# Keys of two groups in one product, and nine more score blocks on VectorE, in a gated mix of two attentions

## The chip, the cores and the metric

One core of a Trainium2 chip. The metric is the device time of one execution in microseconds (us); three executions gave a median of 815.02 (814.9 to 815.13). TensorE multiplies matrices into PSUM, ScalarE does the exponentials, VectorE and GpSimd the elementwise work, and DMAs are issued from SyncE's queue (SP) and GpSimd's.

## The reference

```python
x = A_x                                              # 1 x 2048 x 512, 32 heads of 16
g = _sigmoid((x * gate_w).sum(-1, keepdims=True))
a = _A_ref(x, A_wqkv, A_wo)                          # full attention
b = _B_ref(x, B_wqkv, B_wo)                          # each query sees 8 keys, at distance 0, 2, ... 14
return g * a + (1 - g) * b
```

with, in `_A_ref`,

```python
scores = jnp.einsum("bhqd,bhkd->bhqk", q, k) * (Dh ** -0.5)
p = _softmax(scores, axis=-1)
o = jnp.einsum("bhqk,bhkd->bhqd", p, v)
```

Attention A needs 32 x 2048 x 2048 exponentials. Attention B is small and is done beside it, for the most part on GpSimd.

## The kernel before

**Blocks and periods.** Attention A is cut into blocks: one head, 128 keys, 512 queries. Four heads form a group, and a group with one chunk of 512 queries is a period: 8 groups times 4 chunks are 32 periods of 64 blocks, in order of chunks and, within a chunk, of groups. A block is a score product (32 rows of the array, out of the key tile kt_all and the query tile qt), an exponential, and a value product (17 columns: 16 values and a one that gives the softmax's sum) into the period's accumulator in PSUM.

**Who does the exponential.** Most blocks go to ScalarE, in sets of three and two by turns: the scores land in PSUM rings, one ACTIVATE makes a set of pT from them (qk and ex, L1308 and L1314). `n_dve` (L20) says how many blocks of each period go to VectorE in place of that, in groups of three (d_set, L1218): per block one eviction that turns the scores into the bits of an approximate exponential (p1, tile dt_a or a part of wkv), per group three shifts of that tile (sh, tile pd_a), and per block four value products, with differently weighted values (vd_all), in place of one. In the first eight periods all groups share one buffer dt_a (NDE = 1, L45); later three are in use, two of them in the space of the weights wkv, which is free once all keys and values of attention A are made.

**Keys.** Groups 0 to 7 are needed one after the other in the first eight periods, and so are made along the way. For one group and one of four chunks of 512 keys, k_proj (L644) makes 16 products (mm_k, L378): four slices of x times four heads, each 32 columns wide, placed beside each other in the array. Columns 16 to 31 of a head hold the next head's keys (for the fourth head the group's first again, copied into wk3 by k3, L587). VectorE evicts the result into kt_all and takes the maximum of each row along (an operation that also writes an accumulator; rowc gives the sign). k_bound (L663) takes the maximum over the chunks, exchanges the halves of each head's 32 rows through two small products with permutation matrices (perm), negates, and fills the 16 rows beside each head's keys with the negative bounds. The query tile has the queries in 16 rows and their absolute values in the other 16, so that a score product gives the score less an upper bound of it.

**Queries.** The first two periods have their own product (q_proj). From the third on q_pair (L788) makes the queries of two groups in one full-width product, VectorE casts them (qs) and takes absolute values (qa), two stores put both into DRAM (q_scr, put), and a load for each period brings them into the layout of qt (get).

**Attention B.** b_tile (L880) makes keys, values and queries of 128 positions on TensorE, stores keys and values (kv_scr), gathers the eight neighbours (ksh, vsh, issued by SP) and multiplies and sums on GpSimd, 16 tiles in all.

**Order.** All work is a list of operations with an engine, a duration, a due time, dependencies and buffers; list_schedule (L175) plays it through, and the order in which it starts them becomes the program order of each engine. An operation with a smaller due time goes first; one that uses a shared PSUM bank gets a much earlier one. S0[p] is the planned start of period p (17 us and 0.465 us for each earlier block of ScalarE). Three PSUM banks serve all projections, the scores of VectorE's blocks and the accumulators, of which at most two are alive. The accumulator's transpose accT (po1, L1345) has a due time 100 us or more past everything else's (PO1D, L118). Where TensorE would be idle for too long, zeros (L1472) puts in products of a zero tile z.

Of the kernel before, what the change touches and what calls it, by code (L numbers as in the profile page):

```python
# [9 lines left out]
ALU = mybir.AluOpType  # L10
AX = mybir.AxisListType
FP32 = mybir.dt.float32
BF16 = mybir.dt.bfloat16
# [3 lines left out]

CFG = dict(
    set_sizes=(3, 2),
    n_dve=(3, 3, 6, 6, 6, 9, 9, 9) + (12,) * 24,  # L20
    dve_tiles=4,
    b_start=36.0,
    b_space=(44.0,) * 4 + (47.0,) * 4 + (49.0,) * 8,
# [4 lines left out]
DH = 16  # L28
NG = 8
W = 8  # L30
DIL = 2
QW = 512
# [4 lines left out]
DEXP = -2.0565  # L37
NV = 4
NGR = 3
ROW = QW + 2  # L40
NPT = 3
NGA = 3
# [9 lines left out]
def _ap(base, dims):  # L52
    return bass.AP(tensor=base.tensor, offset=base.offset, ap=[list(d) for d in dims])
# [53 lines left out]
SB = lambda n: [(True, 0.065 + n / 3840.0)]  # L107
# [4 lines left out]
WAVE = lambda n: PASS * n  # L112
# [189 lines left out]
def kernel(  # L302
# [26 lines left out]
    const = ctx.enter_context(tc.tile_pool(name="const", bufs=1))  # L329
# [37 lines left out]
    V = Chained(nc.vector, "dve")  # L367
    A = Chained(nc.scalar, "act")
    G = Chained(nc.gpsimd, "pool")
    SP = Chained(nc.sync, "sp")  # L370

    def mm(out, lhsT, rhs, start, stop, **kw):
        return chain(nc.tensor.matmul(out, lhsT=lhsT, rhs=rhs, start=start, stop=stop, **kw))  # L373
# [16 lines left out]
    def op(eng, occ, fn, dl, **kw):  # L390
        if any(tk.kind == "misc" for tk in kw.get("use", ())):
            dl -= URG[eng]
        o = Op(eng, occ, fn, dl, **kw)
        ops.append(o)
        return o
# [17 lines left out]
    n_dve = cfg["n_dve"]  # L413
# [43 lines left out]
    S0 = [T0 + UNIT * f for f in first_unit]  # L457

    wkv = const.tile([128, DC, 2 * D], BF16, name="wkv")
    wq = const.tile([128, DC, D], BF16, name="wq")  # L460
    wq2 = const.tile([128, DC, 8, 2, DH], BF16, name="wq2")
    q_scr = tc.dram_tile([NG * NC // 2 * 16, DH * QW], BF16, name="q_scr")
    wk3 = const.tile([128, DC, NG, 2, DH], BF16, name="wk3")
    a_w3 = A_wqkv.rearrange("(c p) n -> p c n", p=128)
    gw = const.tile([128, DC], BF16, name="gw")
    bw = const.tile([128, DC, 3 * D], BF16, name="bw")
    bwo = const.tile([128, DC, D], BF16, name="bwo")
# [7 lines left out]
    rowc = const.tile([128, 3], FP32, name="rowc")  # L475
    wts = const.tile([128, NV - 1], BF16, name="wts")
    z32 = const.tile([128, 32], BF16, name="z32")
    z_bc = _ap(z32[:, 0:1], [list(z32[:].ap[0]), [0, QW]])
    perm = const.tile([128, 2, 4, 2, DH], BF16, name="perm")
    qmask = const.tile([128, 1], U32, name="qmask")  # L480
    xT = const.tile([128, DC, S], BF16, name="xT")
    kt_all = const.tile([128, NG, S], BF16, name="kt_all")
    vp_all = const.tile([128, NT, H, DH + 1], BF16, name="vp_all")
    vd_all = const.tile([128, NV - 1, NTD, H, DH + 1], BF16, name="vd_all")
    kmax_all = const.tile([128, NG, NC], FP32, name="kmax_all")
    kmax_b = const.tile([128, NG], BF16, name="kmax_b")
    negk = const.tile([128, NG], FP32, name="negk")
# [29 lines left out]
    def init_perm():  # L517
        idv = ident[:].rearrange("p (a b d) -> p a b d", a=4, b=2)
        G.memset(perm[:], 0.0)
        G.tensor_copy(out=perm[:, 0, :, 1, :], in_=idv[:, :, 0, :])  # L520
        G.tensor_copy(out=perm[:, 1, 1:4, 1, :], in_=idv[:, 0:3, 1, :])
        G.tensor_copy(out=perm[:, 1, 0, 1, :], in_=idv[:, 3, 1, :])

    def init_pool2():
        make_identity(nc, identf)
# [11 lines left out]
    o_perm = op("pool", 1.0, init_perm, -8.5, deps=[o_id])  # L537
    o_init_p = op("pool", 2.8, init_pool2, -8.0, deps=[o_perm])
# [37 lines left out]
    o_wk = op("sp", 0.5, load_w(1), -8.9, lat=6.5)  # L576
# [10 lines left out]
    def k3(E, i0, i1):  # L587
        def s():
            wk = wkv[:, :, 0:D].rearrange("p c (i j d) -> p c i j d", i=NG, j=4)
            for e, j in ((0, 3), (1, 0)):  # L590
                E.tensor_copy(out=wk3[:, :, i0:i1, e, :], in_=wk[:, :, i0:i1, j, :])
        return s
# [6 lines left out]
        return s  # L599

    o_k3 = [op("dve", 0.2, k3(V, 0, 1), -4.0, deps=[o_wk])]
    o_k3 += [op("pool", 2.0, k3(G, 1, NG), -3.0, deps=[o_wk, o_init_p])] * (NG - 1)
    o_q2 = [op("dve", 0.5, q2(V, 0), 0.0, deps=[o_wq]), op("pool", 1.5, q2(G, 1), 5.0, deps=[o_wq, o_k3[1]])]

    def warm():
# [5 lines left out]
    o_xt = []  # L611
    for sc in range(NC):
        st = {}
# [76 lines left out]
            o_k[i] = [op("dve", 0.0, fill(0, S), dl, deps=[c], parts=SB(S))] * NC  # L690

    o_k = {}
    for i in range(NG):
        o_kc[i] = []
        for sc in range(NC):
            if i == 0:
                o_kc[i].append(k_proj(i, sc, ("misc", "acc", "misc", "misc")[sc], -2.0 + sc))
            else:
                o_kc[i].append(k_proj(i, sc, "misc", S0[i] - 14.0 - 3.5 * (NC - 1 - sc), rel=S0[i - 1] - 12.0 if i > 1 else K1REL))
        k_bound(i, 2.0 if i == 0 else S0[i] - 11.0)  # L700
# [87 lines left out]
    def q_pair(pi, dl, rel):  # L788

        c_, i = periods[pi]  # L790
        st = {}
        tk, tqs, tqa = tok("misc", 2), tok("qs", 1), tok("qa", 1)

        def part(c0, c1):
            def s():
                if c0 == 0:
                    st["p"] = misc_ps([128, QW])
                for c in range(c0, c1):
                    mm(st["p"][:], wq[:, c, 4 * i * DH:4 * (i + 2) * DH], xT[:, c, c_ * QW:(c_ + 1) * QW], c == 0, c == DC - 1)
            return s  # L800

        def ev():
            st["s"] = work.tile([128, QW], BF16, name="qs", tag="qs", bufs=1)
            V.tensor_copy(out=st["s"][:], in_=st["p"][:])

        def ab():
            st["a"] = work.tile([128, QW], BF16, name="qa", tag="qa", bufs=1)
            V.tensor_scalar(out=st["a"][:].bitcast(U32), in0=st["s"][:].bitcast(U32), scalar1=0x7FFF7FFF, scalar2=None,
                            op0=ALU.bitwise_and)

        def put(e):
            def s():
                src = st["sa"[e]]
                SP.dma_start(out=_ap(q_scr[8 * pi + e:8 * pi + e + 1, :], [[2 * DH * QW, 8], [QW, DH], [1, QW]]),
                             in_=src[:])
            return s

        def get(e):
            def s():
                qt_tiles[pi + e] = work.tile([128, QW], BF16, name="qt", tag="qt", bufs=4)  # L820
                SP.dma_start(out=qt_tiles[pi + e][:], in_=_ap(q_scr[8 * (pi + e):8 * (pi + e) + 1, :], [[QW, 128], [1, QW]]))
            return s
        a = op("pe", WAVE(2), part(0, 2), dl - 8.6, full=2, deps=[o_wq] + o_xt[c_], alloc=[tk], rel=rel, name=f"qp{pi}")
        a = op("pe", WAVE(2), part(2, DC), dl - 8.0, full=2, deps=[a], use=[tk], name=f"qp{pi}")
        c = op("dve", 0.61, ev, dl - 7.0, deps=[a], alloc=[tqs], use=[tk])
        b = op("dve", 0.0, ab, dl - 6.8, deps=[c], alloc=[tqa], use=[tqs], parts=SB(QW))
        w = [op("sp", 0.5, put(0), dl - 5.0, deps=[c], use=[tqs], lat=2.2), op("sp", 0.5, put(1), dl - 4.0, deps=[b], use=[tqa], lat=2.2)]
        for e in range(2):
            q_tok[pi + e] = tok("qt", 4)
            o_q[pi + e] = op("sp", 0.5, get(e), dl - 1.0 + e, deps=w, alloc=[q_tok[pi + e]], lat=2.2)  # L830
# [468 lines left out]
    for k, us in enumerate(sets):  # L1299
# [6 lines left out]
        st = dict(k=k, us=us, tn=tn, tp=tp)  # L1306
# [7 lines left out]
        def ex(st=st, n=n, k=k):  # L1314
# [4 lines left out]
        a = op("pe", 0.0, qk, tn - 3.0, mode="r", js=[u_[2] for u_ in us], deps=[o_q[pi] for pi in pis] + kd,  # L1319
               alloc=[tr_], use=[q_tok[pi] for pi in pis], after=[last_qk[0]], scores=k % 2, name=f"qk{k}")  # L1320
# [15 lines left out]
    for pi, (c_, i) in enumerate(periods):  # L1336
        st = {}
# [179 lines left out]
```

## Time and profile before

| | |
|---|---|
| median of three runs | 815.02 us |
| profiled execution | 816.37 us |
| its span, first to last instruction | 814.6 us |
| mean granted TensorE clock | 0.997 |
| first pT on ScalarE starts | 18.54 us |
| pT instructions on ScalarE | 778.7 us busy, 684 instructions, 1709 blocks |
| TensorE, products of the zero tile | 138.2 us, 425 |
| keys: products of wkv and of wk3 (tile wk) | 384 and 128 |
| evictions of keys out of PSUM | 32, from 10.0 to 197.2 us |

The profile's columns: a group line has the source line, engine, operation, output and input tiles with their shapes and count, then busy time and mean ns of one, then the idle time just ahead of them on their engine and what ended it. L364 and L373 are helpers that record every instruction, so the tile's name tells what a line is. Matmuls overlap: the start of the next one says more than the duration.

### The profile page before, as it was taken

The numbers are of one execution on the slowest core, as the hardware profiler recorded it, in microseconds if no ns is written. First come the engines' busy times: TensorE is split into PE (matmuls) and PEld (weight loads), VectorE is DVE, ScalarE is ACT, GpSimd is POOL, SyncE is SP. The second block draws the span as 40 slices with busy tenths as digits, with TensorE's granted clock in tenths as the row PEclk, the third lists the DMA queues.
The fourth block names the chain that finished last, engine by engine and source line by source line (L and its number), as shares of the span: only waits on it lengthen the run. The fifth ranks groups of instructions, "written<-read, shape, count | busy, mean of one in ns | idle before, by whom it ended". The sixth has DMA issues, their size and how long they took to land.

```text
span 814.6 us, 18016 instructions
## 1 busy us (share of the span) xinstructions
PE 754.1 (93%) x6969; PEld 247.2 (30%) x7022; DVE 685.0 (84%) x1068; ACT 786.8 (97%) x708; POOL 633.1 (78%) x1058
## 2 busy tenths in 40 slices
PE   8989999999999999989899999899989998999997
PEld 5343333323222222222232222223222222322322
DVE  5636787787988999989988899998989699999796
ACT  3999999999999999999999999999999999999996
POOL 3097979997998999999997894979789219998910
PEclk9999999999999999999999999999999999999999
DMA  8503081544344354444524516162442321522000
GB/s 261 140 5 118 2 180 42 149 111 104 93 100 127 104 118 130 110 112 107 132 54 111 136 33 163 34 162 54 91 130 50 81 86 58 144 59 72 1 2 27
DMA packets 58886, 77.22 MB, mean 95 GB/s; under 512 B 3744, under 2 KB 50848, under 8 KB 58800
## 3 DMA queue, kind: packets, MB, share of 16 engines
q1 hardware_dynamic: 52608, 53.91, 21.4%
q0 software_dynamic: 6048, 22.02, 14.8%
q8 instruction: 55, 0.90, 0.5%
q14 instruction: 31, 0.25, 0.1%
q10 hardware_dynamic: 144, 0.13, 0.0%
HBM read 43.78 MB, written 10.26 MB: 66 GB/s over the span
## 4 chain that ended last, share of the span: by engine, by line
ACT 49%; PE 24%; issue 21%; DVE 3%; DMA 2%; SPq 1%; ACTq 0%; DVEq 0%
ACT pT L364 48%; PE misc_ps L373 16%; PE ring L373 8%; DMA xld<-in_A_x_dram 1%; ACT lg L364 1%; SPq L364 1%; DMA woarr<-in_A_wo_dram 0%; DVE pd_a L364 0%; DMA q_scr<-qa 0%; DVE accT L364 0%; PE pxt L621 0%; DVE qs L364 0%; DVE qa L364 0%; DVE kt_all L364 0%; DVE kvs L364 0%
## 5 line engine op out<-in xcount | busy, mean ns | idle before, releaser
L364 ACT ACTIVATE pT<-ring 128x1536 bf16<-128x1536 f32 (+1 forms) x684 | 778.7, 1329 | 12.1 <-PE ring L373 9.3
L373 PE MATMUL ring<-qt,kt_all 32*128 32x512 bf16 x1709 | 268.7, 382 | 46.7 <-ACT pT L364 39.0
L364 POOL TENSOR_TENSOR prod<-ksh,qb 128x256 f32<-128x256 bf16 x256 | 174.0, 729 | 58.0 <-DMA ksh<-kv_scr 53.2
L373 PE MATMUL misc_ps<-pT,vp_all 128*17 128x512 bf16 (+1 forms) x1709 | 205.6, 384 | 1.7 <-DVE accT L364 1.1
L373 PEld LDWEIGHTS <-kt_all 32*128 32x128 bf16 x2048 | 88.2, 91 | 294.9 <-issue 286.4
L364 DVE TENSOR_SCALAR pd_a<-wkv 128x1536 uint16<-128x1536 uint16 x192 | 175.0, 941 | 0.9 <-PE misc_ps L373 0.4
L364 POOL TENSOR_TENSOR prod<-prod 128x256 f32<-128x256 f32 (+1 forms) x256 | 167.2, 668 | 5.6
L364 DVE TENSOR_SCALAR wkv<-misc_ps 128x512 uint16<-128x512 f32 x192 | 128.7, 683 | 26.8 <-PE misc_ps L373 24.1
L373 PE MATMUL misc_ps<-z 128*32 128x512 bf16 x425 | 138.2, 387 | 1.6 <-DVE z L364 1.6
L364 DVE TENSOR_SCALAR pd_a<-dt_a 128x1536 uint16<-128x1536 uint16 x147 | 135.2, 943 | 1.8 <-PE misc_ps L373 1.1
L373 PE MATMUL misc_ps<-pd_a,vd_all 128*17 128x512 bf16 x1017 | 130.9, 381 | 0.4 <-DVE pd_a L364 0.2
L373 PE MATMUL misc_ps<-qt,kt_all 32*128 32x512 bf16 x339 | 124.2, 381 | 1.3 <-DVE kt_all L364 0.4
L364 DVE TENSOR_SCALAR dt_a<-misc_ps 128x512 uint16<-128x512 f32 x147 | 98.8, 683 | 26.6 <-PE misc_ps L373 25.0
L364 POOL TENSOR_TENSOR prod<-vsh,lg 128x256 f32<-128x256 bf16 x128 | 84.2, 758 | 0.0
L373 PEld LDWEIGHTS <-vp_all 128*17 128x17 bf16 (+1 forms) x2048 | 55.1, 88 | 87.0 <-issue 73.2
L364 POOL TENSOR_TENSOR av<-vsh,lg 128x256 f32<-128x256 bf16 x128 | 78.2, 646 | 0.0
L373 PE MATMUL misc_ps<-bw,xT 128*128 128x512 bf16 x164 | 51.7, 389 | 1.1 <-issue 0.5
L373 PEld LDWEIGHTS <-z 128*32 128x32 bf16 x425 | 37.5, 96 | 48.2 <-issue 24.8
L373 PEld LDWEIGHTS <-vd_all 128*17 128x17 bf16 x1017 | 34.5, 88 | 48.2 <-issue 39.4
L373 PEld LDWEIGHTS <-xT 128*128 128x128 bf16 x576 | 29.1, 97 | 34.0 <-issue 31.0
L373 PE MATMUL misc_ps<-xT,wkv 128*32 128x512 bf16 x384 | 36.6, 381 | 0.0
L373 PE MATMUL misc_ps<-xT,wk 128*32 128x512 bf16 x128 | 35.8, 381 | 0.0
(89 smaller groups left out, 554.0 us busy)
## 6 DMA issues: line engine op xcount, KB each, us to landing
ksh<-kv_scr SPq DMA_DIRECT2D x32, 512.0 KB
vsh<-kv_scr SPq DMA_DIRECT2D x32, 512.0 KB
av<-prod POOLq DMA_DIRECT2D x28, 512.0 KB, 5.7
av<-av POOLq DMA_DIRECT2D x14, 512.0 KB, 5.3
kv_scr<-kvs SPq DMA_DIRECT2D x16, 256.0 KB
qt<-q_scr SPq DMA_DIRECT2D x30, 128.0 KB
q_scr<-qs SPq DMA_DIRECT2D x15, 128.0 KB
q_scr<-qa SPq DMA_DIRECT2D x15, 128.0 KB
```

The costliest lines, as they stand in the source:

```text
L364: return chain_on(key, f(*a, **k))
L373: return chain(nc.tensor.matmul(out, lhsT=lhsT, rhs=rhs, start=start, stop=stop, **kw))
```

## The change

Three things. The blocks of VectorE in the fifth to eighth period go from 6, 9, 9, 9 to 9, 9, 12, 12 (339 to 348 in all). The keys of groups 2 to 7 are made in pairs: the weights of two groups are interleaved into wkp by GpSimd at the start (per head position 16 columns of the one group, then 16 of the other), and one product, 128 columns wide, takes the place of eight. The eviction into the even group's tile is as before; the odd group's tile is made from that tile in SBUF, with the sign turned (KSB). One maximum covers both (so it is the largest absolute value), the exchange takes two small products for the pair, and then each group's tile gets its fill, in which the rows of the other group's keys are overwritten by the bounds. In the odd group the keys lie in the second 16 rows of each 32, so the queries and absolute values of odd groups are stored the other way round, which takes two stores of 64 partitions in place of one of 128.

```diff
-    n_dve=(3, 3, 6, 6, 6, 9, 9, 9) + (12,) * 24,
+    n_dve=(3, 3, 6, 6, 9, 9, 12, 12) + (12,) * 24,
...
+NK1 = 2
+KSB = True
+KPD, KPS, KPR, KP1, KP2 = 16.0, 3.5, 20.0, 44.0, 11.0
...
-    wk3 = const.tile([128, DC, NG, 2, DH], BF16, name="wk3")
+    wk3 = const.tile([128, DC, NK1, 2, DH], BF16, name="wk3")
+    wkp = const.tile([128, DC, (NG - NK1) // 2, 4, 2, DH], BF16, name="wkp")
...
-    perm = const.tile([128, 2, 4, 2, DH], BF16, name="perm")
+    perm = const.tile([128, 3, 4, 2, DH], BF16, name="perm")
...
+        G.tensor_copy(out=perm[:, 2, :, 0, :], in_=idv[:, :, 1, :])
...
-    o_k3 += [op("pool", 2.0, k3(G, 1, NG), -3.0, deps=[o_wk, o_init_p])] * (NG - 1)
+    o_k3 += [op("pool", 0.6, k3(G, 1, NK1), -3.0, deps=[o_wk, o_init_p])] * (NK1 - 1)
+
+    def kpw():
+        wk = wkv[:, :, 4 * NK1 * DH:D].rearrange("p c (i e j d) -> p c i e j d", e=2, j=4, d=DH)
+        for c in range(DC):
+            for e in range(2):
+                G.tensor_copy(out=wkp[:, c, :, :, e, :], in_=wk[:, c, :, e, :, :])
+    o_kp = op("pool", 2.0, kpw, 6.0, rel=12.0, deps=[o_wk, o_k3[1]])
...
+    def k_pair(i, dl, rel):
+        cs = []
+        for sc in range(NC):
+            st = {}
+            tk = tok("misc", 2)
+            def part(c0, c1, st=st, sc=sc):
+                def s():
+                    if c0 == 0:
+                        st["p"] = misc_ps([128, QW])
+                    for c in range(c0, c1):
+                        mm(st["p"][:], wkp[:, c, (i - NK1) // 2].rearrange("p j e d -> p (j e d)"), xT[:, c, sc * QW:(sc + 1) * QW],
+                           c == 0, c == DC - 1)
+                return s
+            def ev(e, st=st, sc=sc):
+                def s():
+                    src = kt_all[:, i, sc * QW:(sc + 1) * QW] if e and KSB else st["p"][:]
+                    V.tensor_scalar(out=kt_all[:, i + e, sc * QW:(sc + 1) * QW], in0=src, scalar1=(1.0, -1.0)[e], scalar2=None,
+                                    op0=ALU.mult, op1=ALU.max, accum_out=kmax_all[:, i + e, sc:sc + 1])
+                return s
+            d = dl - KPS * (NC - 1 - sc)
+            a = op("pe", WAVE(2), part(0, 2), d - 1.8, full=2, deps=[o_kp] + o_xt[sc], alloc=[tk], rel=rel, name=f"kp{i}.{sc}")
+            a = op("pe", WAVE(2), part(2, DC), d - 1.2, full=2, deps=[a], use=[tk], name=f"kp{i}.{sc}")
+            a = op("dve", 0.61, ev(0), d, deps=[a], use=[tk])
+            cs += [a, op("dve", 0.61, ev(1), d + 0.3, deps=[a], use=[] if KSB else [tk])]
...
+        def mx():
+            V.tensor_reduce(out=kmax_b[:, i:i + 1], in_=kmax_all[:, i:i + 2, :], axis=AX.XY, op=ALU.max)
+        def sw():
+            st["p"] = misc_ps([128, 2])
+            for e in range(2):
+                mm(st["p"][:, e:e + 1], perm[:, 2 * e].rearrange("p a b d -> p (a b d)"), kmax_b[:, i:i + 1], True, True)
+        def ng():
+            V.tensor_scalar(out=negk[:, i:i + 2], in0=st["p"][:], scalar1=-1.0, scalar2=None, op0=ALU.mult)
+        def fill(e):
+            def s():
+                V.tensor_scalar(out=kt_all[:, i + e, :], in0=kt_all[:, i + e, :], scalar1=rowc[:, 1 + e:2 + e],
+                                scalar2=negk[:, i + e:i + e + 1], op0=ALU.mult, op1=ALU.add)
+            return s
...
+        for e in range(2):
+            o_k[i + e] = [op("dve", 0.0, fill(e), dl + 3.0 + 20.0 * e, deps=[m], parts=SB(S))] * NC
+
+    for i in range(NK1, NG, 2):
+        k_pair(i, S0[i] - (KPD if i > 2 else KP2), S0[i - 1] - KPR if i > 2 else KP1)
+    for i in range(NK1):
...
         def put(e):
             def s():
                 src = st["sa"[e]]
+                if i < NK1:
-                SP.dma_start(out=_ap(q_scr[8 * pi + e:8 * pi + e + 1, :], [[2 * DH * QW, 8], [QW, DH], [1, QW]]),
-                             in_=src[:])
+                    SP.dma_start(out=_ap(q_scr[8 * pi + e:8 * pi + e + 1, :], [[2 * DH * QW, 8], [QW, DH], [1, QW]]),
+                                 in_=src[:])
+                    return
+                for g_ in range(2):
+                    r0 = 8 * (pi + g_) + (e ^ g_)
+                    SP.dma_start(out=_ap(q_scr[r0:r0 + 1, :], [[2 * DH * QW, 4], [QW, DH], [1, QW]]),
+                                 in_=src[64 * g_:64 * g_ + 64, :])
```

The due times of a pair: its last chunk is planned 16 us (11 for groups 2 and 3) ahead of the start of the even group's first period, and none of its products ahead of 20 us before the period in front (44 us for groups 2 and 3). Before, a group's last chunk was due 14 us ahead of its own period.

More of the change, by code (lines that the diff above doesn't have):

```diff
@@ L692 @@
     o_k = {}
-    for i in range(NG):
+    def k_pair(i, dl, rel):
[22 more added lines that the diff above has]
+            cs += [a, op("dve", 0.61, ev(1), d + 0.3, deps=[a], use=[] if KSB else [tk])]
+        st = {}
+        tk = tok("misc", 2)
+        def mx():
[11 more added lines that the diff above has]
+            return s
+        m = op("dve", 0.2, mx, dl + 0.5, deps=cs)
+        m = op("pe", 0.1, sw, dl + 1.0, full=0, deps=[m, o_perm], alloc=[tk])
+        m = op("dve", 0.2, ng, dl + 1.8, deps=[m], use=[tk])
+        for e in range(2):
+            o_k[i + e] = [op("dve", 0.0, fill(e), dl + 3.0 + 20.0 * e, deps=[m], parts=SB(S))] * NC
@@ L826, in q_pair @@
         b = op("dve", 0.0, ab, dl - 6.8, deps=[c], alloc=[tqa], use=[tqs], parts=SB(QW))
-        w = [op("sp", 0.5, put(0), dl - 5.0, deps=[c], use=[tqs], lat=2.2), op("sp", 0.5, put(1), dl - 4.0, deps=[b], use=[tqa], lat=2.2)]
+        np_ = 0.5 if i < NK1 else 1.0
+        w = [op("sp", np_, put(0), dl - 5.0, deps=[c], use=[tqs], lat=np_ + 1.7),
+             op("sp", np_, put(1), dl - 4.0, deps=[b], use=[tqa], lat=np_ + 1.7)]
         for e in range(2):
```

## The prediction

> **What bounds the kernel now.** I read the busy times first, then the span in stretches, then ScalarE's own timeline with its gaps, then what TensorE did just ahead of the gaps.
>
> The first line of the page says that ScalarE is the bound:
>
> ```profile
> PE 754.1 (93%) x6969; PEld 247.2 (30%) x7022; DVE 685.0 (84%) x1068; ACT 786.8 (97%) x708; POOL 633.1 (78%) x1058
> ```
>
> TensorE's 93% is softer than it looks: 138.2 us of it are fillers (the 425 products of the zero tile z). The stretches show when ScalarE is short of work (columns: stretch, length, busy us and count on PE, PEld, DVE, ACT, POOL, then granted clock, DMA share, GB/s):
>
> ```profile
> 100.00:125.00 25.00, 23.83 (x265) 8.21 (x263) 21.13 (x38) 23.52 (x22) 19.04 (x31) 1.00 0.69 159
> 150.00:175.00 25.00, 23.16 (x245) 7.14 (x240) 18.97 (x35) 23.49 (x23) 23.90 (x39) 0.93 0.50 109
> 225.00:250.00 25.00, 23.38 (x184) 6.65 (x186) 20.82 (x31) 25.00 (x24) 20.88 (x36) 1.00 0.54 137
> 275.00:300.00 25.00, 24.10 (x212) 7.25 (x213) 24.59 (x38) 24.95 (x24) 24.00 (x40) 1.00 0.64 148
> ```
>
> From 175 us on ScalarE has hardly a hole, though periods of 12 VectorE blocks run there. Before, it loses about a microsecond in each stretch. The holes on its timeline (start, length, instruction, idle before it and who ended that):
>
> ```profile
> 54.54 5.97 ACT L364 ACTIVATE pT<-ring 128x1536 bf16<-128x1536 f32 x5 [1.45 <-PE misc_ps L373]
> ...
> 83.37 6.89 ACT L364 ACTIVATE pT<-ring 128x1536 bf16<-128x1536 f32 x6 [0.86 <-PE ring L373]
> ...
> 107.27 2.37 ACT L364 ACTIVATE pT<-ring 128x1536 bf16<-128x1536 f32 x2 [1.19 <-PE ring L373]
> ...
> 136.59 13.66 ACT L364 ACTIVATE pT<-ring 128x1536 bf16<-128x1536 f32 x12 [1.00 <-PE ring L373]
> ...
> 167.97 12.87 ACT L364 ACTIVATE pT<-ring 128x1536 bf16<-128x1536 f32 x11 [1.38 <-PE ring L373]
> ```
>
> With two small ones (0.26 at 68.55, 0.29 at 112.56) that is 6.43 us in seven gaps, all ended by TensorE. Ahead of the gap at 136.59 TensorE was making keys:
>
> ```profile
> 134.49 0.58 PE L373 MATMUL misc_ps<-xT,wkv 128*32 128x512 bf16 x3
> 134.70 0.38 PE L373 MATMUL misc_ps<-xT,wk 128*32 128x512 bf16 x1
> 134.71 0.58 PE L373 MATMUL misc_ps<-xT,wkv 128*32 128x512 bf16 x3
> ...
> 136.09 0.60 PE L373 MATMUL ring<-qt,kt_all 32*128 32x512 bf16 x5
> ...
> 163.39 0.40 PE L373 MATMUL misc_ps<-pT,vp_all 128*32 128x512 bf16 x4 [1.10 <-DVE accT L364]
> ```
>
> Four products 32 wide run beside each other, and the next four start 0.22 us later (134.49 to 134.71). Eight such waves, group 5's last two chunks, fill 133.84 to 135.57, and only behind them come the scores that ScalarE waits for. The last line is another kind of gap: TensorE waits 1.10 us for VectorE's transpose accT, and then its clock halves:
>
> ```profile
> 164.00:166.00 2.00, 2.00 (x10) 0.35 (x7) 1.35 (x4) 1.89 (x3) 1.64 (x3) 0.56 0.84 129
> 166.00:168.00 2.00, 2.00 (x16) 0.32 (x15) 1.76 (x4) 0.62 (x2) 2.00 (x4) 0.59 0.28 94
> ```
>
> So up to 175 us the bound is ScalarE plus TensorE's crowding, and after it ScalarE alone. The costs on VectorE:
>
> ```profile
> L364 DVE TENSOR_SCALAR pd_a<-dt_a 128x1536 uint16<-128x1536 uint16 x147 | 135.2, 943 | 1.8 <-PE misc_ps L373 1.1
> L373 PE MATMUL misc_ps<-pd_a,vd_all 128*17 128x512 bf16 x1017 | 130.9, 381 | 0.4 <-DVE pd_a L364 0.2
> L364 DVE TENSOR_SCALAR dt_a<-misc_ps 128x512 uint16<-128x512 f32 x147 | 98.8, 683 | 26.6 <-PE misc_ps L373 25.0
> L364 DVE TENSOR_SCALAR_CACHE_REDUCE kt_all<-misc_ps,rowc 128x512 bf16<-128x512 f32 x32 | 23.8, 745 | 12.7 <-PE misc_ps L373 12.5
> ```
>
> **Part by part.** *Blocks.* The periods add up to 339 blocks on VectorE before and 348 after, so ScalarE does 1700 blocks instead of 1709. Its group of pT takes 778.7 us for 1709, 0.4557 us a block; nine fewer are **-4.10 us**, and ScalarE is the path, so they count in full if nothing else becomes short. 1700 is a whole number of sets of 3 and 2; the last set then has two blocks instead of one, which is in the 0.4557.
>
> The price on VectorE is three groups more, each of three evictions (683 ns) and three shifts (943 ns): 3 x 4.88 = 14.6 us by single durations; in the 186 to 236 us stretch six groups took 28.3 us (11.05 + 17.28, the busy time of dt_a's instructions), 4.72 each. On TensorE each block adds a score product of its own and three more value products. Of the latter three run side by side, at the 0.22 us of a wave: 9 x 0.22 = 2.0 us, and 9 x 0.22 = 2.0 at most for the scores, some of which ride beside the ring's. VectorE is busy 79.3 us of the 98 in 131 to 229 us (72%, 82%, 79% and 90% in its four periods), so 18.7 us are free for the 14.6: room on the whole, but not in the last of them (second rival).
>
> *Keys on TensorE.* Six groups x 4 chunks x 4 waves x 0.215 us = 20.6 us become three pairs x 4 x 4 full-width products at 0.213 (two wq products take 0.60 us, one 0.39) = 10.2 us: 10.4 us less, minus the 4.0 above, 6.4 us net, nearly all between 50 and 200 us. TensorE's time isn't the bound; it counts only where it ends a gap. The gaps at 83.37 and 136.59 (0.86 + 1.00) have the keys of groups 3 and 5 right ahead, which now come with 2 and 4 up to a period sooner: **-1.86 us**. For 107.27 and 112.56 it is group 4's keys; the pair's products take as long as group 4's did and keep a due time near theirs (16 against 14 us ahead of the period), so I leave both. The gap at 54.54 waits for value products whose values were cast only at 52.67, and 167.97 for the clock: left too.
>
> *Keys on VectorE.* 24 evictions remain, 12 of them now from the bf16 keys in SBUF. No row shows that operation. Bounds: 0.83 us (the same operation out of PSUM, 0.745 + 0.082), and 0.35 us (the plain fill of 512 from SBUF, 1.38 us for four). I take the upper end, being the same operation: nothing saved; the lower end would free 12 x 0.48 = 5.8 us of VectorE, off the path. Three maxima (0.16) and three negations (0.21) go: 1.1 us. The fills are as many as before, and group 5's and 7's are due some 7 us into the period ahead of their own.
>
> *GpSimd.* The start has two copies of 448 elements (0.56 each) less 384, and eight of 192 more: between 0.23 (64 elements) and 0.40 (256) each, say 0.34, so 2.7 - 0.7 = +2.0 us. They fit into the 4.71 us in which GpSimd waits for wq after 7.46 us; if they took double, wq's copies would come a microsecond late, and these are first used near 40 us. One copy and a longer memset of perm (+0.3 us) fall ahead of that. Nothing on the path.
>
> *Queues.* 12 of the 15 query pairs split both stores in two: 24 more issues on SP at 0.58 us. A pair's loads wait one or two issues longer, about 1.2 us; for the pair stored from 209.64 they went out at 217.72 for a period that began near 236. What queues behind them on SP are the gathers ksh and vsh for GpSimd, which ends its work at 776 us, 30 us ahead of ScalarE. No cost; without that cover it would be 12 x 1.2 = 14 us on GpSimd's chain.
>
> *New gaps.* The order is planned afresh, with VectorE fuller where it was short of waits. I allow one new gap of the mean size, 6.43 / 7 = **+0.92 us** (bounds: none, and three halvings of the clock like 164 to 168 us, 3 x 1.38 = 4.1).
>
> **Sum:** -4.10 - 1.86 + 0.92 = -5.04 us. Against the profiled execution: span 814.6 to 809.6, with the 1.8 us around it 816.4 to 811.3. That execution lies 1.35 us above the median 815.02, so the median should come to **810.0**.
>
> **Rivals.**
> *All gaps but the one at 54.54 close*, because 6.4 us of TensorE time leave the crowded stretch: 815.02 - 4.10 - 4.98 = 805.9. For it: every gap is ended by TensorE. Against: 167.97 is VectorE's doing and VectorE gets fuller.
>
> *VectorE becomes the bound in the seventh and eighth period.* Up to there all groups share one buffer (NDE = 1), so a group's first eviction waits for the last shift of the one before. In 186 to 236 us VectorE was busy 43.4 us: 28.3 for six groups, 15.1 for the rest, of which 2.0 for group 7's keys move ahead. After: 8 x 4.72 + 13.1 = 50.9 us in 104 x 0.4557 = 47.4 us: 3.5 us over, and 10.1 with the 6.6 us that it idled there. The accumulator's transpose has the latest due time on VectorE, so it goes last, TensorE stands at the first value product as at 163.39, and the clock halves. If all 10.1 us reach ScalarE: 815.02 - 5.96 + 10.1 = 819.2, and it is slower than before once more than 5.96 us do. Against: two accumulators exist, so ScalarE stops only when a period ends with the one before not yet transposed; at 292.46 us accT started some 8 us into a period (565 blocks and the gaps behind 18.54 us), and ScalarE lost 0.05 us in that stretch. That a halving needs little is in the rows: a wait of 1.10 us came ahead of one, and 1.38 us of ScalarE went with it. The Trainium skill ("TensorE: Matmul & The Clock Gate", "Why this matters for your kernels") says that the clock falls after idle gaps of more than about 3 us between bursts. By that rule this rival's waits would leave the clock alone up to 3 us and its time would be the overrun alone; the trace does not agree (1.10 us sufficed there), so the rival keeps its chance.
>
> *Half of that:* some 5 us reach ScalarE, and the time stays within 0.2% (1.6 us) of before, about what a measurement of this kernel can tell from no change: 815.
>
> *The keys' relief buys nothing* (TensorE fills the freed time with other projections that also stand ahead of the scores): 815.02 - 4.10 + 0.92 = 811.8, up to 813.3 with another halving.
>
> **Chances.** Forecast (808 to 811.8) 0.50; all gaps close (below 808) 0.17; relief buys nothing (811.8 to 813.4) 0.13; no change 0.09; slower 0.11. So faster 0.80, same 0.09, slower 0.11. The range 806 to 815 leaves out the slower case, part of no change, and the lowest end of the gaps' case, about 0.2.
>
> **What would show it.** ACT's pT at about 774.6 us of busy time; no gap where groups 3 and 5 had their keys; the 48 full-width products of wkp at 0.21 us a piece; ScalarE full from 175 us on. Wrong would be: gaps of several microseconds in ScalarE between 180 and 250 us, an accT more than 20 us into the next period, or a clock below 0.9 in several stretches.

## The result and the profile after

| | before | after |
|---|---|---|
| median | 815.02 us (814.9 to 815.13, five runs) | 811.55 us (810.31 to 812.36, five runs) |
| profiled execution, its span | 816.37, 814.6 | 811.55, 809.7 |
| mean granted TensorE clock there | 0.997 | 0.995 |
| pT busy on ScalarE | 778.7 us | 775.0 us |
| ScalarE idle between its first and last pT | 7.66 us | 6.53 us |
| products of z | 425 | 412 |

The idle time is the stretch from the start of the first pT to the end of the last one, less ScalarE's busy time in it, small gaps included. The ratio is 0.9956, with an interval of 0.9943 to 0.9969. The changed kernel is faster by 3.5 us, and the forecast of 810.0 is 1.5 us low.

The busy times of the changed kernel, its groups that the prediction priced (the trace has 45 of the 48 products of wkp), and its 25-us stretches (columns as before: length, then busy time and count on PE, PEld, DVE, ACT and POOL, granted clock, DMA share, GB/s):

```profile
PE 744.5 (92%) x6637; PEld 241.5 (30%) x6694; DVE 695.4 (86%) x1080; ACT 782.8 (97%) x704; POOL 633.0 (78%) x1067
```

```profile
L376 PE MATMUL misc_ps<-xT,wkp 128*128 128x512 bf16 x45 | 13.3, 383 | 0.2 <-issue 0.2
L367 DVE TENSOR_SCALAR_CACHE_REDUCE kt_all<-misc_ps 128x512 bf16<-128x512 f32 x12 | 8.2, 684 | 3.1 <-PE misc_ps L376 3.1
L367 DVE TENSOR_SCALAR_CACHE_REDUCE kt_all<-kt_all 128x512 bf16<-128x512 bf16 x12 | 8.0, 675 | 0.1
L367 POOL COPY wkp<-wkv 128x192 bf16<-128x192 bf16 x8 | 2.4, 344 | 0.0
```

```profile
100.00:125.00 25.00, 23.34 (x222) 8.91 (x221) 20.66 (x38) 25.00 (x24) 20.02 (x32) 1.00 0.60 142
150.00:175.00 25.00, 23.95 (x217) 8.90 (x217) 23.50 (x43) 25.00 (x24) 24.00 (x37) 1.00 0.57 137
225.00:250.00 25.00, 21.90 (x164) 6.28 (x162) 20.05 (x28) 23.20 (x22) 20.55 (x34) 0.93 0.54 127
275.00:300.00 25.00, 23.17 (x198) 6.56 (x200) 24.45 (x37) 24.91 (x23) 17.08 (x29) 1.00 0.45 117
```

Before, the first two of these stretches had ScalarE at 23.52 and 23.49 us, and the third at 25.00. After, the first two are full and the third has lost 1.8 us. The crowded part of the kernel was mended, and a new hole opened where there was none. ScalarE's timeline shows the same (start, length, instruction, idle before it and who ended that):

```profile
54.66 5.97 ACT L367 ACTIVATE pT<-ring 128x1536 bf16<-128x1536 f32 x5 [1.47 <-PE misc_ps L376]
...
234.44 1.02 ACT L367 ACTIVATE pT<-ring 128x1024 bf16<-128x1024 f32 x1 [0.58 <-PE ring L376]
235.96 1.45 ACT L367 ACTIVATE pT<-ring 128x1536 bf16<-128x1536 f32 x1 [0.50 <-PE ring L376]
237.86 1.02 ACT L367 ACTIVATE pT<-ring 128x1024 bf16<-128x1024 f32 x1 [0.45 <-PE ring L376]
239.15 1.45 ACT L367 ACTIVATE pT<-ring 128x1536 bf16<-128x1536 f32 x1 [0.27 <-PE ring L376]
...
568.14 2.37 ACT L367 ACTIVATE pT<-ring 128x1536 bf16<-128x1536 f32 x2 [1.02 <-PE misc_ps L376]
```

Of the seven gaps of before only the first is left: 6.43 us have become 1.47. A gap of 0.21 us at 212.10 has gone too. New are 1.80 us at 234 to 239, 0.65 at 265 and 268, 1.22 at 568 and 571, and 0.44 at 660: 4.11 us. pT is 3.7 us shorter, where nine blocks at 0.4557 would make 4.10. So the account from profile to profile is -3.7 - 4.96 - 0.21 + 4.11 = -4.76, against the -4.9 us by which the span changed.

What opened the hole at 234 stands on three engines. TensorE waits 1.88 us for accT; VectorE makes accT late because the instruction ahead of it, qa, took 2.50 us; and beside qa GpSimd did four products in a row. In the order PE, DVE, POOL of the timeline:

```profile
231.65 0.39 PE L376 MATMUL ring<-qt,kt_all 32*128 32x512 bf16 x3
233.92 0.37 PE L376 MATMUL misc_ps<-qt,kt_all 32*128 32x512 bf16 x1 [1.88 <-DVE accT L367]
```

```profile
230.75 2.50 DVE L367 TENSOR_SCALAR qa<-qs 128x256 uint32<-128x256 uint32 x1
233.17 0.70 DVE L367 STREAM_TRANSPOSE accT<-misc_ps 128x512 f32<-128x512 f32 x1
```

```profile
230.37 2.71 POOL L367 TENSOR_TENSOR prod<-vsh,lg 128x256 f32<-128x256 bf16 x4
```

The fifteen qa of this run take between 0.278 and 2.496 us, so this one stood still for about 2.2 us, and it ended when GpSimd's row did (230.75 + 2.50 = 233.25, 230.37 + 2.71 = 233.08). The Trainium skill ("SBUF — State Buffer", "Who interferes with whom") says that VectorE in its two-port modes and GpSimd lock each other out of a shared pair of ports, whole instructions long. The trace fits that, though no row shows in which mode qa ran, and it adds that VectorE did not get in between the four products. Behind the wait the clock is halved, in the 2-us stretches:

```profile
232.00:234.00 2.00, 0.12 (x6) 0.07 (x2) 2.00 (x3) 1.85 (x2) 1.70 (x3) 1.00 0.81 204
234.00:236.00 2.00, 2.00 (x16) 0.38 (x16) 1.35 (x4) 1.06 (x2) 0.89 (x3) 0.56 1.08 232
236.00:238.00 2.00, 2.00 (x14) 0.44 (x10) 1.97 (x3) 1.55 (x2) 2.00 (x4) 0.59 1.04 218
```

TensorE is busy 0.12 us of the first stretch; then two at 0.56 and 0.59 of the clock, and ScalarE, which had lost 0.15 us, loses 0.94 and 0.45. Here the wait costs little by itself, and the slow TensorE behind it costs most.

### The profile page after: what moved, and what is told of

It is laid out like the page before. It is cut to its first block, busy times and chain, and to the rows that moved or that the text cites. A ratio compares the mean times of both kernels' runs of the same rounds, so it can differ in the third digit from the quotient of the medians.

```text
span 809.7 us, 17412 instructions
## 1 busy us (share of the span) xinstructions
PE 744.5 (92%) x6637; PEld 241.5 (30%) x6694; DVE 695.4 (86%) x1080; ACT 782.8 (97%) x704; POOL 633.0 (78%) x1067
## 4 chain that ended last, share of the span: by engine, by line
ACT 49%; PE 27%; issue 20%; DVE 2%; DMA 1%; SPq 0%; ACTq 0%
ACT pT L367 49%; PE misc_ps L376 18%; PE ring L376 8%; DMA xld<-in_A_x_dram 1%; DVE pd_a L367 1%; ACT lg L367 1%; DVE accT L367 0%; PE pxt L633 0%; DVE kt_all L367 0%; DVE wkv L367 0%; DVE dt_a L367 0%; ACT xT L367 0%; SPq L367 0%; DVE qa L367 0%; DVE oat L367 0%
## 5 line engine op out<-in xcount | busy, mean ns | idle before, releaser
L367 ACT ACTIVATE pT<-ring 128x1536 bf16<-128x1536 f32 (+1 forms) x680 | 775.0, 1331 | 10.9 <-PE ring L376 7.3
L376 PE MATMUL ring<-qt,kt_all 32*128 32x512 bf16 x1700 | 268.7, 383 | 48.0 <-ACT pT L367 40.4
L367 POOL TENSOR_TENSOR prod<-ksh,qb 128x256 f32<-128x256 bf16 x256 | 171.5, 726 | 46.0 <-DMA ksh<-kv_scr 35.5
L376 PEld LDWEIGHTS <-kt_all 32*128 32x128 bf16 x2048 | 90.6, 91 | 301.9 <-issue 294.0
L367 POOL TENSOR_TENSOR prod<-prod 128x256 f32<-128x256 f32 (+1 forms) x256 | 169.7, 679 | 5.2
L367 DVE TENSOR_SCALAR pd_a<-dt_a 128x1536 uint16<-128x1536 uint16 x156 | 142.6, 941 | 3.5 <-PE misc_ps L376 2.7
L376 PE MATMUL misc_ps<-pd_a,vd_all 128*17 128x512 bf16 x1044 | 135.1, 382 | 0.6 <-DVE pd_a L367 0.5
L376 PE MATMUL misc_ps<-qt,kt_all 32*128 32x512 bf16 x348 | 128.7, 382 | 4.3 <-DVE accT L367 2.1
L367 DVE TENSOR_SCALAR dt_a<-misc_ps 128x512 uint16<-128x512 f32 x156 | 104.5, 683 | 23.8 <-PE misc_ps L376 21.7
L376 PE MATMUL misc_ps<-wkv,vp_all 128*17 128x512 bf16 x192 | 31.5, 384 | 0.0
L367 DVE CAST kvs<-misc_ps 128x512 bf16<-128x512 f32 x32 | 21.9, 684 | 10.8 <-PE misc_ps L376 10.8
```

The costliest lines, as they stand in the source:

```text
L367: return chain_on(key, f(*a, **k))
```

## The experiments

**The two halves of the change, each alone.** The theory of the prediction: blocks and keys both count, and each shows alone. The rival: the keys' relief buys nothing. The first kernel is the changed one with the blocks of before:

```diff
-    n_dve=(3, 3, 6, 6, 9, 9, 12, 12) + (12,) * 24,
+    n_dve=(3, 3, 6, 6, 6, 9, 9, 9) + (12,) * 24,
```

> The keys in pairs alone, blocks as before (339). Theory A (the pairs closed the gaps between 60 and 170 us by themselves): those gaps are gone, ScalarE's pT stay at 778.7 us, and the time is 815.0 - 3.6 = 811.4 us (4.96 us of gaps less the 1.38 us of the gap with the halved clock, which the typical execution of before need not have), within 1 us for halvings elsewhere. Rival (they closed because nine blocks left ScalarE): the gaps stay, 814 to 815 us.

Measured: 811.13 us (810.2 to 812.04), ratio 0.9955 [0.9942, 0.9967]. The keys alone bring as much as the whole change. ScalarE's line on the page and its only gap before 290 us:

```profile
L367 ACT ACTIVATE pT<-ring 128x1536 bf16<-128x1536 f32 (+1 forms) x684 | 777.7, 1347 | 7.0 <-PE ring L376 4.6
```

```profile
54.56 20.45 ACT L367 ACTIVATE pT<-ring 128x1536 bf16<-128x1536 f32 x18 [1.45 <-PE misc_ps L376]
```

The same 1709 blocks as before take 1.0 us less, and the idle time between the first and the last pT falls from 7.66 to 2.57. That is 6.0 of the 6.2 us by which the span is shorter than the profiled one of before (808.4 against 814.6); the profiled execution is the fastest of the five here. The rival has fallen. From here to the changed kernel pT falls by 2.7 us and the idle time rises by 4.0: **the nine blocks, on top of the keys, bring nothing**, by the medians as by the fastest runs (810.2 and 810.31 us). What no run separates is which part of the new keys closes the gaps: the halved time of their products on TensorE, or the earlier due times that came with it.

This kernel also shows that a held qa does not open a hole by itself. VectorE has one of 2.06 us here, in the same place and beside four products of GpSimd (229.63 to 232.36), with accT behind it:

```profile
230.46 2.06 DVE L367 TENSOR_SCALAR qa<-qs 128x256 uint32<-128x256 uint32 x1
233.04 0.70 DVE L367 STREAM_TRANSPOSE accT<-misc_ps 128x512 f32<-128x512 f32 x1
```

TensorE had other products to do meanwhile and waited for no other engine longer than 0.31 us, and ScalarE lost nothing. In the changed kernel TensorE's next product waited for accT itself, the 1.88 us above.

The second kernel is the one of before with the blocks of after, the same line turned round.

> The blocks alone (348), keys as before. Theory A: ScalarE's pT at 774.6 us (-4.1), but gaps of 5 us or more stay between 50 and 175 us and grow by the added products on TensorE, and the single buffer's groups make new ones up to 240 us: 811.5 to 814 us. Rival (the pairs are not needed for the gain, the blocks alone bring it): 811 us or less with no more gaps than before.

Measured: 838.48 us (834.36 to 839.9), ratio 1.0272 [1.0249, 1.0294], far outside what either theory expected. ScalarE, VectorE and TensorE in this kernel:

```profile
303.00 2.36 ACT L364 ACTIVATE pT<-ring 128x1536 bf16<-128x1536 f32 x2 [12.40 <-PE misc_ps L373]
```

```profile
301.41 0.72 DVE L364 STREAM_TRANSPOSE accT<-misc_ps 128x512 f32<-128x512 f32 x1
```

```profile
294.56 0.37 PE L373 MATMUL misc_ps<-qt,kt_all 32*128 32x512 bf16 x1 [0.78 <-DVE dt_a L364]
295.71 0.37 PE L373 MATMUL misc_ps<-qt,kt_all 32*128 32x512 bf16 x1 [0.78 <-DVE dt_a L364]
...
302.19 0.71 PE L373 MATMUL misc_ps<-pT,vp_all 128*32 128x512 bf16 x4
```

This is the prediction's slower rival nearly to the letter: both accumulators in use, accT only at 301.41, and ScalarE stopped for 12.40 us. While they are in use one bank is left for VectorE's scores, so each score waits for the eviction ahead of it (0.78 us, one every 1.15 us), and ScalarE's value products come only at 302.19. The accT at 301.41 is the ninth; the ninth stood at 271.42 before and at 267.08 after. Counted from ScalarE's last pT of the period, the seventh, eighth and ninth accT come 15, 22 and 41 us late here, 2, 2 and 10 before, and 5, 6 and 14 after. The stop makes 12.40 of the 28.3 us that ScalarE is idle here. So these blocks, in these periods, weren't to be had with the old keys. What made accT late stays open: VectorE was not full (busy 15.01 of 25 us from 262.5 to 287.5), and from 154 us on none of its instructions took 0.9 us more than the shortest of its kind.

**The instruction that stands still.** Theory: qa beside GpSimd opens the hole at 234; a qa that isn't held back closes it. Rival: without it VectorE is late anyway. In the first attempt qa is cut into two instructions of 16-bit elements whose patterns don't match (three runs out, six in), to keep it from sharing:

```diff
-            V.tensor_scalar(out=st["a"][:].bitcast(U32), in0=st["s"][:].bitcast(U32), scalar1=0x7FFF7FFF, scalar2=None,
-                            op0=ALU.bitwise_and)
+            for n0, n1 in ((0, 510), (506, 512)):
+                o_, i_ = st["a"][:].bitcast(U16)[:, n0:n1], st["s"][:].bitcast(U16)[:, n0:n1]
+                k_ = (n1 - n0) // 6
+                V.tensor_scalar(out=_ap(o_, [list(o_.ap[0]), [2 * k_, 3], [1, 2 * k_]]),
+                                in0=_ap(i_, [list(i_.ap[0]), [k_, 6], [1, k_]]), scalar1=0x7FFF, scalar2=None,
+                                op0=ALU.bitwise_and)
```

> The changed kernel with every engine's order as it is, but the absolute values qa are taken by two VectorE instructions whose input and output patterns differ in shape (as the shifts' do), so that they should not have to wait for GpSimd. Theory A (the gaps of 1.80 us at 234 to 240 us come from one qa that took 2.50 us ahead of the accumulator's transpose): no qa over 0.7 us, TensorE's wait for accT at 232 us under 0.6 us instead of 1.88, full clock there, 811.5 - 1.8 = 809.7 us. Rival (VectorE is simply late there, with 12 blocks a period on one buffer): the wait stays over 1 us, the clock halves, 811.5 us.

Measured: 812.86 us (810.72 to 816.21), ratio 0.9973 [0.9961, 0.9985]. The edit failed as a lever: the two instructions took 3.46 us at 230.77, again beside four products of GpSimd (231.23 to 233.86). It gives a second dose instead. TensorE in this kernel:

```profile
234.90 0.58 PE L376 MATMUL misc_ps<-qt,kt_all 32*128 32x512 bf16 x1 [2.84 <-DVE accT L367]
```

With the same order of instructions the wait is 2.84 us for 1.88, and ScalarE's four gaps there are 3.84 us for 1.80.

In the second attempt qa is max(-q, q), read out of PSUM right behind qs:

```diff
+            st["a"] = work.tile([128, QW], BF16, name="qa", tag="qa", bufs=1)
+            V.scalar_tensor_tensor(out=st["a"][:], in0=st["p"][:], scalar=-1.0, in1=st["s"][:], op0=ALU.mult, op1=ALU.max)
...
-            V.tensor_scalar(out=st["a"][:].bitcast(U32), in0=st["s"][:].bitcast(U32), scalar1=0x7FFF7FFF, scalar2=None,
-                            op0=ALU.bitwise_and)
```

> The changed kernel with TensorE's order as it is; the absolute values qa are made out of PSUM (the larger of the negated product and of qs), right behind qs, so that only one input lies in SBUF. The variant x_qa did not keep qa from waiting, so it left the question open. Theory A (the wait for accT at 232 us, and the halved clock behind it, come from qa waiting for GpSimd): qa at 0.7 us every time, TensorE's wait for accT under 0.6 us, no gap of ScalarE at 234 to 240 us, 811.5 - 1.8 = 809.7 us, with the gaps of 0.65 us at 265 us and 0.44 at 660 still there. Rival (VectorE is late there with 12 blocks on one buffer, whatever qa does): a wait of over 1 us stays and 811.5 us with it.

Measured: 812.57 us (811.39 to 815.95), ratio 0.9975 [0.9965, 0.9986]. The tile qa in this kernel (min/median/max in ns, then who waited for it, in us and times):

```profile
L367 DVE SCALAR_TENSOR_TENSOR qa<-misc_ps,qs x15: 691/691/692, 22.3 to 718.9; 128x512 bf16<-128x512 f32 x15
...
  PE misc_ps L376: 3.7, 8
```

The local claim holds: no qa is ever held back, ScalarE has no gap between 225 and 263 us, and the clock isn't halved at 234. But the time is no lower, and not the 809.7 expected. qa now keeps the PSUM bank, and TensorE waits eight times for it, 3.7 us in all. A gap of 1.08 us appears at 271, behind a halving that begins at 268.7. qa also stands earlier in VectorE's order here, no longer right ahead of accT, so the run shows that the hole goes when qa is out of accT's way, not that the shorter qa alone would do.

**Which periods the blocks go to.** Theory: it is the full seventh and eighth period that costs; the same 348 blocks spread out cost less (on record this stands as the rival). Rival: where they stand doesn't matter. The edit is in the changed kernel, alone and together with the qa out of PSUM:

```diff
-    n_dve=(3, 3, 6, 6, 9, 9, 12, 12) + (12,) * 24,
+    n_dve=(3, 3, 9, 9, 9, 9, 9, 9) + (12,) * 24,
```

> The changed kernel with the same 348 blocks spread as 3, 3, 9, 9, 9, 9, 9, 9: no period of 12 on one buffer. Rival (12 blocks on one buffer make VectorE late): no gap in 225 to 245 us, 809.7 us. Theory A (it is the collision of one qa, which a new order moves at random): gaps of 1 to 3 us in all, but anywhere, 809 to 812 us; periods 3 and 4 have room for 9 blocks, since the pairs left TensorE time there.

Measured: 809.76 us (808.56 to 810.37), ratio 0.9932 [0.992, 0.9944]. VectorE and ScalarE in the stretch of the hole, in this kernel:

```profile
225.00:250.00 25.00, 23.12 (x177) 6.70 (x175) 15.14 (x24) 25.00 (x24) 20.07 (x34) 1.00 0.67 163
```

VectorE is busy 15.14 us for 20.05, ScalarE is full, and the clock is 1.00. It beats the changed kernel by 1.8 us between medians. The idle time is 5.15 us, still 2.6 above that of the kernel with 339 blocks. Both expectations on record allow for this time, so it doesn't tell the full periods from a collision that a new order moved: qa took 0.39 us here, at 227.19, and accT came four microseconds behind it.

> The same qa out of PSUM in the kernel with blocks 3, 3, 9, 9, 9, 9, 9, 9. Theory A: that kernel's remaining halving (at 257 to 261 us) has no qa ahead of it, so qa changes little: 809.5 us, within 0.8 us of x_even. If qa's waits cost in general, 808.5 us or less.

Measured: 814.48 us (813.18 to 817.14), ratio 0.9993 [0.9983, 1.0004], against the expectation. The new qa costs 4.7 us here, of which TensorE's direct waits for it are 2.7 (six times). The remainder stays open; that the order was planned for a bank that comes free sooner is only argued.

> The changed keys, qa out of PSUM, and 354 blocks as 3, 3, 9, 9, 9, 9, 12, 12. Theory A (ScalarE's instructions get 0.456 us a block shorter and TensorE has room in the third and fourth period): 2.7 us less of ScalarE than x_qp, given back in part as gaps: 807.5 to 809.5 us. Rival (TensorE is the next bound, so that fewer blocks on ScalarE only turn into waiting): 809.7 us or more.

Here n_dve is 3, 3, 9, 9, 9, 9, 12, 12 (354 blocks), with the qa out of PSUM. Measured: 813.01 us (812.46 to 815.66), ratio 0.9981 [0.9972, 0.999]. That is the rival's side. pT is down to 774.0 us and the idle time up to 7.86, with the clock at 0.999: blocks can be given back as plain waiting too, with hardly a halving. The same 354 blocks with the qa of the changed kernel:

> The changed keys with 354 blocks: 3, 3, 9, 9, 9, 9, 12, 12, with qa as in the changed kernel. Theory C: 809.8 - 2.7 = 807.1 us if the periods of 12 on one buffer did no harm; as they did in the changed kernel, 808.5 to 810.5 us. Rival (VectorE and TensorE are full): 811 us or more.

Measured: 809.29 us (808.81 to 811.12), ratio 0.9933 [0.9921, 0.9945], as expected. This and the even 348 are the fastest kernels here, and their runs overlap. This one has twelve blocks in the seventh and the eighth period like the changed kernel, and yet ScalarE is busy for all of 212.5 to 237.5 us: full periods don't open the hole at 234 by themselves. Whether they cost something elsewhere stays open, for six blocks more than in the even kernel bring 0.5 us here and not 2.7.

**How many blocks.** Theory: with the new keys a block costs ScalarE's 0.456 us up to some number and nothing beyond it. Rival: the planned order, which is drawn afresh each time, moves the time by more than a few blocks do. In the changed kernel, 3, 3, 6, 6, 6, 6, 6, 9 (333) and 3, 3, 6, 9, 9, 9, 9, 9 (345):

> The changed keys with six blocks fewer on VectorE than before (333: 3, 3, 6, 6, 6, 6, 6, 9). Theory C (with the pairs, ScalarE is the bound at 339 blocks): six blocks more on ScalarE cost 6 x 0.456 = 2.7 us over x_keys, 813.9 us, in a run without gaps past 60 us. Rival (TensorE or VectorE is the bound at 339 already): 811 us, as with 339.

> The changed keys with 345 blocks: 3, 3, 6, 9, 9, 9, 9, 9. Theory C (a block moved saves 0.456 us as long as no period has 12 blocks on one buffer): 811.1 - 2.7 = 808.4 us. Rival (past 339 the saving is given back by waits of TensorE on VectorE): 810 to 812 us.

Measured: 815.45 us (813.34 to 820.67), ratio 1.0012 [0.9995, 1.0028], and 813.49 us (811.62 to 819.32), ratio 0.9991 [0.9975, 1.0008]. In order of the number of blocks, with the new keys and the old qa:

| blocks on VectorE | 333 | 339 | 345 | 348 (changed) | 348 (even) | 354 |
|---|---|---|---|---|---|---|
| median, us | 815.45 | 811.13 | 813.49 | 811.55 | 809.76 | 809.29 |
| pT busy, us | 780.8 | 777.7 | 775.7 | 775.0 | 775.3 | 773.3 |
| ScalarE idle inside, us | 2.90 | 2.57 | 5.54 | 6.53 | 5.15 | 7.72 |

The two lower rows are of the profiled executions, which took 813.84, 810.2, 811.62, 811.55, 810.37 and 811.12 us. pT falls with the blocks, the even 348 apart. Up to 339 the idle time stays put, and six blocks gain about what pT falls by: 3.1 us there, and 3.1 between the fastest runs of the two (813.3 and 810.2). Past 339 the idle time takes up most of it. But 345 is slower than its neighbours on both sides, where both expectations had it lower, and the two 348 lie 1.8 us apart: the rival holds for steps this small. Why 345 is slow stays open.

**With the old keys, less at a time.** The kernel of before with 342 blocks, one group more in the fifth period:

```diff
-    n_dve=(3, 3, 6, 6, 6, 9, 9, 9) + (12,) * 24,
+    n_dve=(3, 3, 6, 6, 9, 9, 9, 9) + (12,) * 24,
```

> The kernel before (keys group by group) with blocks 3, 3, 6, 6, 9, 9, 9, 9: three more than before, none of the periods of 12 on one buffer. Theory B (in x_blocks, 12 blocks in a period on one buffer, beside keys of groups 6 and 7, made VectorE's groups late until ScalarE stopped for 12.4 us): no gap over 3 us, 812.5 to 815.5 us. Rival (any block more than before is too many with the old keys): a gap of over 5 us again, 820 us or more.

Measured: 818.61 us (817.06 to 820.45), ratio 1.0043 [1.0027, 1.006]. Slower, but without a stop like the 12.40 us; neither theory had that. VectorE, TensorE and ScalarE show what it is instead:

```profile
149.21 3.81 DVE L364 TENSOR_SCALAR kt_all<-kt_all,rowc,negk 128x2048 bf16<-128x2048 bf16 x1
```

```profile
154.60 0.58 PE L373 MATMUL misc_ps<-qt,kt_all 32*128 32x512 bf16 x1 [2.61 <-DVE kt_all L364]
```

```profile
155.72 2.51 ACT L364 ACTIVATE pT<-ring 128x1536 bf16<-128x1536 f32 x2 [3.09 <-PE ring L373]
```

The fill of a group's keys, 0.81 us for the one at 120.71 in the same run, took 3.81 us, next to four products of GpSimd (149.83 to 152.45). TensorE then waits 2.61 us for the evictions behind it, the clock goes to 0.50 from 154 to 160, and ScalarE loses 3.09 us. It is the mechanism of the hole at 234 with another instruction, in a kernel that has none of the change's new keys. In this kernel and in the one with 348 blocks and the old keys, the gaps at 68, 83, 107, 112 and 136 stand as before (0.26, 0.86, 1.19, 0.29 and 1.09 us): they go with the old keys, whatever the blocks.

**The clock.** Theory: halvings begin where TensorE has thin work, and more fillers prevent them. Rival: fillers stand in the way of real work. In the even kernel the filling aims higher:

```diff
-ROWS_SPAN, ROWS_MIN, ROWS_IDLE, ROWS_ADD, ROW_STRIP = 2.3, 6.5, 8.0, 4, 0.25
+ROWS_SPAN, ROWS_MIN, ROWS_IDLE, ROWS_ADD, ROW_STRIP = 2.3, 7.5, 8.0, 4, 0.25
```

> The kernel x_even with more fillers on TensorE (7.5 full-width products wanted in each 2.3 us, in place of 6.5). Theory D (its spread from 808.6 to 810.4 us comes from the clock's halvings, which too little work on TensorE brings on): clock 0.998 or more in all runs, spread under 0.8 us, median near 808.6 us. Rival (the fillers stand in the way of scores): the clock is full, but the time is 810 us or more.

Measured: 823.78 us (818.57 to 827.22), ratio 1.0105 [1.0079, 1.0132]. The fillers' group in this kernel:

```profile
L376 PE MATMUL misc_ps<-z 128*32 128x512 bf16 x504 | 167.2, 390 | 1.6 <-DVE z L367 1.6
```

504 fillers for 422, 14 us slower, ScalarE idle 20.41 us for 5.15. The clock is lower, not higher (0.982 to 0.995 over the runs), so the theory's forecast has fallen; the rival had the time right and the clock wrong. That the fillers stand in the way is not shown, for the order was planned afresh, and it holds qa up three times where the even kernel has none over 0.85 us:

```profile
157.01 3.09 DVE L367 TENSOR_SCALAR qa<-qs 128x256 uint32<-128x256 uint32 x1
...
210.27 3.19 DVE L367 TENSOR_SCALAR qa<-qs 128x256 uint32<-128x256 uint32 x1
...
247.39 2.78 DVE L367 TENSOR_SCALAR qa<-qs 128x256 uint32<-128x256 uint32 x1
```

All three stand beside rows of GpSimd products. TensorE then waits 2.40, 2.22 and 1.83 us for VectorE, two halvings come with them, and the gaps of ScalarE behind them add up to 8.3 of the 20.4 us. The rest stays open.

## Why the prediction was right or wrong

**Right: direction, and the sum, by misses that cancel.** The sum was -5.04 us of span and the measured one -4.9. That the two agree is luck: two of its three terms were off by more than 3 us, in opposite directions.

**"-1.86" for the keys: right in mechanism, mis-sized.** It is -4.96. Not only the gaps with keys right ahead of them closed (83.37, 136.59), but also 68.55, 107.27, 112.56 and 167.97; only the one at 54 stayed, for which the prediction gave the cause. The kernel with the keys alone, and the two with other blocks and the old keys, show that it is the keys' doing. The rival "all gaps but the one at 54.54 close" priced this at 4.98. The step that failed is to credit the new keys only with the gaps right behind the products that went: every gap of the crowded stretch but that one closed. The rival that the relief buys nothing is refuted.

**"+0.92" for new gaps: mis-sized, 4.11.** That is at the stated upper bound (three times 1.38). The largest of them isn't VectorE short of time on the whole, as the prediction reasoned with its 50.9 us of work in 47.4: it was busy 20.05 of the 25 us around the hole. It is one instruction of VectorE held back 2.2 us beside GpSimd, with accT behind it and TensorE in need of accT.

**"Nine blocks count in full": failed.** The condition "if nothing else becomes short" wasn't met. pT fell by 3.7 us of the 4.10 priced, but against the kernel with the keys alone the time did not fall at all.

**The step to the median: wrong.** The profiled execution of before lay 1.35 us above the median, and the prediction took 1.35 off the forecast as an offset of the measurement. The record points to a gap, the 1.38 us at 167.97 with a halved clock, though no execution of before without it was profiled. Of 17 runs of the kernel before that ran beside the first four experiments, 14 had a clock of 0.999 or more and 814.7 to 815.1 us; the other three 0.996 to 0.998 and 816.2 to 817.5. Against the median, then, -4.9 + 1.38 = -3.5 us, measured -3.47. To take a gap out of the base and leave it in the list of gaps counts it twice as soon as it closes.

**The slower rival: a real mechanism in the wrong kernel.** It rests on a false reading, which the description of the order ahead of the prediction has too: accT's due time is E - 300, with E the planned end of its period, so among VectorE's ready work it goes first, not last. It waits for the period's last value products and for the instruction that runs. In the changed kernel it came 14 us behind ScalarE's last pT of the period at most, and the stop came only with the old keys.

**Prices.** The eviction out of SBUF takes 675 ns, with the 80 ns of reading the accumulator close below the upper end that was taken; the copies of wkp take 344 ns (0.34 expected); the wkp products stand 0.22 us apart back to back (0.21 expected). "ScalarE full from 175 us on" was wrong at 234 and at 568.

## What to carry to other kernels

When one engine is full and another crowds it, cut the crowding work first, as the kernel with the keys alone did; moving work off the full engine afterwards pays only as far as the idle time of the full engine stays put, which is the number to follow beside its busy time. Look along the second engine for instructions that read and write SBUF beside a row of GpSimd work and have something urgent behind them: one of them can cost more than the work that was saved (3.09 us against three blocks at 0.456). And compare the profiled execution's clock and gaps with the other runs before you turn their difference into an offset.

## What the runs showed of the hardware

The clock was halved at or just behind TensorE waits of 1.10 us (before), 1.88 us (after) and 2.61 us (342 blocks with the old keys), but not behind one of 1.83 us (at 250.82, with more fillers). It was also halved without a long wait for another engine: at 268.7 us with qa out of PSUM, behind waits of 0.23 us at most, and at 565.3 us in the changed kernel, behind 0.64 and 0.52 us:

```profile
562.00:564.00 2.00, 1.36 (x18) 0.46 (x16) 0.91 (x2) 2.00 (x3) 1.92 (x4) 1.00 0.02 4
564.00:566.00 2.00, 1.48 (x14) 0.46 (x14) 1.89 (x4) 2.00 (x2) 1.92 (x5) 0.83 0.02 4
566.00:568.00 2.00, 2.00 (x14) 0.45 (x10) 1.01 (x2) 1.11 (x2) 1.92 (x5) 0.50 0.00 0
```

So the rule of about 3 us that the prediction took from the Trainium skill ("TensorE: Matmul & The Clock Gate", "Why this matters for your kernels") does not bound the waits in these runs, and no single wait's length tells a halving. What does stays open. The qa that reads PSUM takes 691 to 692 ns fifteen times over, the one that goes from SBUF to SBUF between 278 and 2496 ns, the longest of them beside a row of GpSimd work; the key evictions from SBUF that also return a maximum took 675 ns in the mean (625 to 687). The Trainium skill ("SBUF — State Buffer", "Who interferes with whom") leaves just that form, with the accumulator written out, out of the two-port modes; the 675 ns agree.
